# Attention and two perceptrons on one core: sums moved between the V products, q and k in one transfer, weights loaded earlier

## The chip, the cores and the metric

The kernel runs on one core of a Trainium2 chip. The metric is device time in microseconds (us) from launch to end. Most of the text speaks of the engines by their short names: PE multiplies matrices, ACT applies functions, DVE and POOL work element by element, SP only issues transfers.

## The reference

Multi-head attention with capped scores, whose output goes through two bias-free perceptrons, all in float32:

```python
batch, n_heads, seq, head_dim = (2, 12, 448, 64)
scores = scale * np.matmul(q, k.transpose(0, 1, 3, 2))
scores = cap * np.tanh(scores / cap)
attn = np.exp(scores - max)            # over the last axis
attn = attn / (np.sum(attn, axis=-1, keepdims=True) + 1e-09)
x = np.matmul(attn, v)                 # heads side by side: (896, 768)
h = x @ w_in;  g = relu(h) ** 2;       x = g @ w_out      # 768 -> 2048 -> 768
h = x @ w2_in; g = h * sigmoid(1.702 * h); out = g @ w2_out
```

The cap bounds the scores, so the kernel takes no maximum.

## The kernel before

**Attention, two heads at a time.** The 24 heads make 12 pairs. A pair's q and k stand transposed with one head on partitions 0 to 63 and the other on 64 to 127. For each pair the kernel makes the scores in three chunks of 128 keys (`scores`) and one of 64 (the first half of `tails`), takes tanh of each chunk (`tanh`, ACT) and one exponential over all of them (`exps`, ACT). The probabilities are multiplied with V chunk by chunk (`weigh`, three chunks c = 0, 1, 2, into the one bank `pv`; the second half of `tails` adds the 64 keys). The row sums come from POOL, which adds the chunks element by element (`add`, four instructions a pair), and from PE, which multiplies the result with a matrix of ones (`sum_up`, into the one bank `sm`). Pair 0 has no `add`: PE sums its chunks directly (`sum_all`). DVE then takes the reciprocal (`invert`, L415), multiplies (`normalise`, L419; it reads `pv`, and the next pair's `weigh` waits for that since there is one such bank) and cuts the result in a high and a low part (`split`, L90 and L93).

**Weights.** Each perceptron product is made of three passes over high and low parts of both factors (`mm3`, L102 to L104). The weights come in 64 blocks of 768 KB (`w.load`), and DVE and ACT turn each into a high and a low part: `magnitude`, `clamp`, `shift`, `low_word` (L151), `sign` (L158), then `high_part` and `low_part` (L90 and L93 on `wa`). The first two blocks are treated wholly inside attention, by `merge` and `parts` on DVE; the third is begun near its end. `w.sign` issues the load of a later block, since it frees the raw buffer.

**The order.** Each engine runs its instructions in the order in which they are written. In attention that order is a list of steps `at(t, fn, ...)`, sorted by the number t; t only sorts, it is no time that the chip keeps. A pair's steps lie PAIR = 6.7 apart. Transfers are issued by SP in the order of the code, but for a few by ACT at the start; a transfer whose buffer is still in use holds up those behind it on SP.

**Start.** ACT loads its function table at its first tanh (L434, on the tile `idle`); WARM matmuls on `idle` follow on PE; then pair 0's k and q arrive, one by SP and one by ACT, behind the tiny transfer of `cap`, from which DVE makes the scale `icap` that the first tanh reads.

**After attention.** `unit_a` for the first 448 rows and two blocks of w_in is run ahead inside attention (`ahead`), between the last pairs' products. Then PE works through 2304 matmuls of the perceptrons with few gaps.

Of the kernel before, what the change touches and what calls it, by code (L numbers as in the profile page):

```python
# [8 lines left out]
F32 = mybir.dt.float32  # L9
# [4 lines left out]
AF = mybir.ActivationFunctionType  # L14
# [5 lines left out]
P = 128  # L20
B, H, S, D = 2, 12, 448, 64
# [18 lines left out]


AHEAD = 2
WARM = 5

PAIR = 6.7


@with_exitstack
def attn_moe_moe(ctx, tc, qT, kT, v, cap, w1i, w1o, w2i, w2o, out):
    nc = tc.nc  # L50
    cp = ctx.enter_context(tc.tile_pool(name="cp", bufs=1))
    xp = ctx.enter_context(tc.tile_pool(name="xp", bufs=1))
# [12 lines left out]
    def sum_bank():  # L65
        return ps.tile([P, 512], F32, tag="sm", name="sm")
# [12 lines left out]
    def bank():  # L79
        return next(ring[0])  # L80
# [3 lines left out]
    def rnd(eng, out_, in_):  # L84
        if eng is nc.scalar:
            nc.scalar.activation(out_, in_, AF.Copy)  # L86
        elif eng is nc.gpsimd:
            nc.gpsimd.tensor_scalar(out_, in_, 1.0, 1.0, op0=ALU.mult, op1=ALU.mult)
        else:
            nc.vector.tensor_copy(out_, in_)  # L90
# [4 lines left out]
    def hi_lo(pool, tag):  # L95
        return (
            pool.tile([P, S], F32R, tag=f"{tag}_h", name=f"{tag}_h"),
            pool.tile([P, S], F32R, tag=f"{tag}_l", name=f"{tag}_l"),
        )
# [214 lines left out]
    def bounded_attention(w, cap_sb, actx):  # L314
        ap_ = actx.enter_context(tc.tile_pool(name="ap", bufs=2))
# [4 lines left out]
        idle = ap_.tile([P, 512], BF16, name="idle", bufs=1)  # L320
        otail = ap_.tile([P, P], F32, name="otail", bufs=1)
        kq, vv, raw, probs, total, sums, pvs, inverse = {}, {}, {}, {}, {}, {}, {}, {}
        halves = (slice(0, D), slice(D, P))
        rows = halves[::-1]

        def load_kq(i):
            b, n = divmod(i, H // 2)
            k = ap_.tile([P, S], F32, tag="k", name="k")
            q = ap_.tile([P, S], F32, tag="q", name="q")
            nc.sync.dma_start(k, kT[b, n])  # L330
            (nc.scalar if i == 0 else nc.sync).dma_start(q, qT[b, n])
            kq[i] = k, q

        def load_v(i):
            b, n = divmod(i, H // 2)
# [85 lines left out]
        def split(i):  # L421
# [3 lines left out]
            rest(nc.vector, ll, u, hh)  # L425
            x[i // 6, i % 6] = hh, ll

        nc.scalar.dma_start(cap_sb, bass.AP(tensor=cap.tensor, offset=cap.offset, ap=[[0, P], [1, 1]]))
        nc.vector.memset(idle, 0.0)
        nc.gpsimd.memset(ones, 1.0 + 1e-9)  # L430
        nc.gpsimd.memset(otail, 0.0)
        for h, r in zip(halves, rows):
            nc.gpsimd.memset(otail[r, h], 1.0 + 1e-9)
        nc.scalar.activation(idle[:, 0:1], idle[:, 1:2], AF.Tanh)  # L434
        warm = sum_bank()
        for _ in range(WARM):
            nc.tensor.matmul(warm, idle[:, :P], idle, start=True, stop=True)
        load_kq(0)
        nc.vector.tensor_scalar(bcap, cap_sb, -CAP_BOUND, CAP_BOUND, op0=ALU.max, op1=ALU.min)
        nc.vector.reciprocal(icap, bcap)  # L440
        nc.vector.tensor_scalar(icap, icap, 1.0 / 8.0, None, op0=ALU.mult)
        load_kq(1)
        w.load()
        load_v(0)

# [2 lines left out]
        def at(t, fn, *args):  # L448
            steps.append((t, fn, *args))

        n = NPR
        for i in range(n):
            t = PAIR * i
            if i > 1:
                at(t - 2 * PAIR + 2.5, load_kq, i)
            if i:
                at(t - 2 * PAIR + 10.3 if i > 2 else 2.6 + 0.2 * i, load_v, i)
            for c, d in enumerate((-5.1, -4.4, -3.7)):
                at(t + d, scores, i, c)
            for c, d in enumerate((-3.5, -3.4, -3.3, 1.0)):  # L460
                at(t + d, tanh, i, c)
            at(t + 3.1, exps, i)
            if i == 0:
                at(t + 6.6, sum_all, i, (0, 1))
                at(t + 8.2, sum_all, i, (2, 3))
            else:
                at(t + 6.6, add, i)
                at(t + {n - 2: 12.3, n - 1: 12.3}.get(i, 13.3), sum_up, i)
            for c, d in enumerate((12.2, 12.4, 12.5) if i == n - 1 else (11.05, 11.8, 12.5)):
                at(t + d, weigh, i, c)  # L470
            at(t + 14.0 if i else 10.4, invert, i)
            at(t + 17.2, normalise, i)
            at(t + 17.9, split, i)
        for i in range(-2, n):
            at(PAIR * i + 14.15 if i > -2 else -3.6, tails, i + 2 if i + 2 < n else None, i if i >= 0 else None)

        at(2.55, w.load)
        def merge(eng):
            w.magnitude(eng)
            w.clamp()  # L480
            w.shift()
            w.low_word()
            w.sign()
# [10 lines left out]
        at(4.0, merge, nc.vector)  # L494
        at(4.1, parts, nc.vector)
        at(9.7, merge, nc.vector)
        at(11.8, parts, nc.vector)
        end = PAIR * (n - 1)
        at(end + 13.0, begin)
        at(end + 13.0, w.low_word)  # L500
        at(end + 18.85, w.sign)
        at(end + 18.9, w.high_part, nc.scalar)
        at(end + 19.05, w.low_part)
# [19 lines left out]
    def general_attention(cap_sb, actx):  # L523
        ap_ = actx.enter_context(tc.tile_pool(name="gap", bufs=2))
        ident = ap_.tile([P, P], F32, name="ident", bufs=1)
        make_identity(nc, ident)
        mag = ap_.tile([P, 1], F32, name="mag", bufs=1)
        icap = ap_.tile([P, 1], F32, name="gicap", bufs=1)
        nc.vector.tensor_scalar(mag.bitcast(U32), cap_sb.bitcast(U32), 0x7FFFFFFF, None, op0=ALU.bitwise_and)
        nc.vector.reciprocal(icap, mag)  # L530
        nc.vector.tensor_scalar(icap, icap, 1.0 / 8.0, None, op0=ALU.mult)
        chunks = [(kc, slice(kc * P, min(S, (kc + 1) * P))) for kc in range(KC + 1)]
        for i in range(NPR):
            b, n = divmod(i, H // 2)
            kq = []
            for nm, src in (("k", kT), ("q", qT)):
                r = ap_.tile([D, 2, S], F32, tag=f"g{nm}", name=f"g{nm}")
                nc.sync.dma_start(r, src[b, n].rearrange("(e d) s -> d e s", e=2))
                kq.append(r)
            k, q = kq  # L540
            vm = ap_.tile([P, 2 * KC, D], F32, tag="gv", name="gv")
            nc.sync.dma_start(vm, v[b, n, :, :2 * KC])
            vl = ap_.tile([TL, 2, D], F32, tag="gvt", name="gvt")
            for e in range(2):
                nc.sync.dma_start(vl[:, e], v[b, n, D * (1 - e):D * (2 - e), 2 * KC])
            u = ap_.tile([P, S], F32, tag="gu", name="gu")
            for e in range(2):
                pT = ap_.tile([P, KC + 1, S], F32, tag="pT", name="pT")
                for qc in range(NC):
                    j = slice(qc * CP, (qc + 1) * CP)  # L550
                    sc = bank()
                    nc.tensor.matmul(sc[:CP, :S], q[:, 1 - e, j], k[:, 1 - e, :], start=True, stop=True)
                    t = ap_.tile([CP, S], F32, tag="gt", name="gt")
                    nc.scalar.activation(t, sc[:CP, :S], AF.Tanh, scale=icap[:CP])
                    m = ap_.tile([CP, 1], F32, tag="gm", name="gm")
                    nc.vector.tensor_reduce(m, t, axis=AX.X, op=ALU.max)
                    nc.vector.tensor_tensor(m, m, mag[:CP], op=ALU.mult)
                    nc.vector.tensor_scalar(t, t, mag[:CP], None, op0=ALU.mult)
                    nc.vector.tensor_scalar(t, t, m, None, op0=ALU.subtract)
                    nc.scalar.activation(t, t, AF.Exp)  # L560
                    s = ap_.tile([CP, 1], F32, tag="gs", name="gs")
                    nc.vector.tensor_reduce(s, t, axis=AX.X, op=ALU.add)
                    nc.vector.tensor_scalar(s, s, 1e-9, None, op0=ALU.add)
                    nc.vector.reciprocal(s, s)
                    nc.vector.tensor_scalar(t, t, s, None, op0=ALU.mult)
                    tp = bank()
                    for kc, jj in chunks:
                        nc.tensor.transpose(tp[:jj.stop - jj.start, kc * CP:(kc + 1) * CP], t[:, jj], ident[:CP, :CP])
                    nc.vector.tensor_copy(pT[:, 0:KC, j], tp[:, :KC * CP].rearrange("p (k q) -> p k q", k=KC))
                    nc.vector.tensor_copy(pT[:TL, KC, j], tp[:TL, KC * CP:S])  # L570
                pv = bank()
                for kc in range(KC):
                    nc.tensor.matmul(pv[:D, :S], vm[:, 2 * kc + e, :], pT[:, kc, :], start=kc == 0, stop=False)
                nc.tensor.matmul(pv[:D, :S], vl[:, e, :], pT[:TL, KC, :], start=False, stop=True)
                nc.scalar.activation(u[D * e:D * e + D, :], pv[:D, :S], AF.Copy)
            hh, ll = hi_lo(xp, f"x{b}_{n}")
            rnd(nc.gpsimd, hh, u)
            rest(nc.gpsimd, ll, u, hh)
            x[b, n] = hh, ll

    cap_sb = cp.tile([P, 1], F32, name="cap_sb")
    w = Weights()
# [8 lines left out]
    with tc.If(mag > CAP_BOUND_BITS):  # L591
        ring[0] = all_banks()
        w = Weights()
# [65 lines left out]
```

## Time and profile before

| | us |
|---|---|
| median of 3 runs | 575.86 |
| lowest and highest of them | 575.0 and 579.22 |
| the profiled execution's own time | 580.23 |
| its span, first to last instruction | 578.4 |
| mean granted PE clock | 0.992 of full |
| busy: PE, DVE, ACT, POOL | 557.5, 386.1, 258.8, 73.5 |

The busy shares are means over stages with different limits: POOL works in attention alone, and PE's busy time counts each matmul until its modelled end. The profiled execution is one run, and it is longer than all three of the timed ones. On PE a float32 matmul is recorded as two passes, so six instructions of the order stand as x12 in the profile.

### The profile page before, as it was taken

The page shows a single profiled execution, that of the slowest core. Times are in us where ns is not written, and L with a number is a line of the kernel's source. Part 1 is how long each engine was busy: PE and PEld are TensorE (multiplying, and loading weights), DVE is VectorE, ACT ScalarE, POOL GpSimd, SP SyncE. Part 2 cuts the span into 40 slices and gives each one's busy share as a digit, 9 for nine tenths or more (in the row PEclk, how much of TensorE's full clock was granted, in tenths as well). Part 3 has the DMA queues.
Part 4 walks back from the last instruction along what each step waited for, and adds up shares of the span by engine and source line. Part 5 has one row for each costly group of instructions (what it writes and reads, how often), then busy time and mean ns, then how long its engine had stood idle before and what let it go on. Part 6 is the DMA issues. An engine that isn't in the chain of part 4 may idle for free.

```text
span 578.4 us, 6902 instructions
## 1 busy us (share of the span) xinstructions
PE 557.5 (96%) x2753; PEld 463.6 (80%) x2753; DVE 386.1 (67%) x523; ACT 258.8 (45%) x333; POOL 73.5 (13%) x52
## 2 busy tenths in 40 slices
PE   6869999999999999999999999999999999999995
PEld 2323334689999999999999999999999999999995
DVE  4666666879988888653775367878888875366401
ACT  4948887055555554321332155555555522222101
POOL 0459999300000000000000000000000000000000
PEclk9979999999999999999999999999999999999999
DMA  5623330034433333431253123232323154154002
GB/s 169 233 86 96 95 97 17 1 110 124 150 109 110 109 110 109 164 110 54 94 179 110 54 98 120 97 123 91 128 83 136 54 172 148 63 199 150 22 0 101
DMA packets 16313, 61.87 MB, mean 107 GB/s; under 512 B 1936, under 2 KB 8080, under 8 KB 16272
## 3 DMA queue, kind: packets, MB, share of 16 engines
q1 hardware_dynamic: 15984, 61.12, 32.0%
q8 instruction: 23, 0.38, 0.3%
q10 hardware_dynamic: 288, 0.23, 0.1%
q14 instruction: 18, 0.15, 0.1%
HBM read 58.59 MB, written 2.75 MB: 106 GB/s over the span
## 4 chain that ended last, share of the span: by engine, by line
PE 86%; DVE 10%; DMA 2%; ACT 1%; issue 1%; SPq 0%; ACTq 0%; DVEq 0%
PE bb L102 19%; PE bb L104 19%; PE bb L103 19%; DVE r L415 5%; PE pv L379 5%; PE pv L103 3%; PE sm L104 3%; PE sm L102 3%; PE pv L104 3%; PE sm L103 3%; PE pv L102 3%; PE sm L396 2%; DMA wraw<-w1i 1%; DVE sm L419 1%; DVE wl L93 1%; DMA q<-qT 1%
## 5 line engine op out<-in xcount | busy, mean ns | idle before, releaser
L102 PE MATMUL bb<-x_l,wh 128*128 128x448 f32 x288 | 105.5, 366 | 0.0
L103 PE MATMUL bb<-x_h,wl 128*128 128x448 f32 x288 | 105.3, 366 | 0.0
L104 PE MATMUL bb<-x_h,wh 128*128 128x448 f32 x288 | 105.2, 365 | 0.0
L104 PE MATMUL bb<-g_h,wh 128*128 128x448 f32 x288 | 105.2, 365 | 0.0
L102 PE MATMUL bb<-g_l,wh 128*128 128x448 f32 x288 | 105.2, 365 | 0.0
L103 PE MATMUL bb<-g_h,wl 128*128 128x448 f32 x288 | 105.2, 365 | 0.0
L86 ACT ACTIVATE wh<-wa 128x768 fp32r<-128x768 f32 x62 | 52.4, 846 | 100.0 <-PE bb L104 45.2
L93 DVE TENSOR_TENSOR wl<-wa,wh 128x768 fp32r<-128x768 f32 x64 | 63.8, 997 | 46.2 <-ACT wh L86 46.1
L132 ACT ACTIVATE wa<-wraw 128x768 f32<-128x768 f32 x62 | 56.6, 913 | 70.2 <-DVE wl L93 16.9
L158 DVE SCALAR_TENSOR_TENSOR wa<-wraw,wa 128x768 uint32<-128x768 uint32 x64 | 62.8, 981 | 1.0
L151 DVE SCALAR_TENSOR_TENSOR wa<-wraw,wa 128x768 uint32<-128x768 uint32 x64 | 60.9, 952 | 0.1
L102 PEld LDWEIGHTS bb<-x_l,wh 128*128 128x128 f32 x288 | 54.1, 188 | 6.4 <-issue 1.4
L103 PEld LDWEIGHTS bb<-x_h,wl 128*128 128x128 f32 x288 | 54.1, 188 | 4.7 <-DVE wl L93 0.4
L104 PEld LDWEIGHTS bb<-x_h,wh 128*128 128x128 f32 x288 | 54.1, 188 | 4.3
L104 PEld LDWEIGHTS bb<-g_h,wh 128*128 128x128 f32 x288 | 54.1, 188 | 4.3
L103 PEld LDWEIGHTS bb<-g_h,wl 128*128 128x128 f32 x288 | 54.1, 188 | 4.3
L102 PEld LDWEIGHTS bb<-g_l,wh 128*128 128x128 f32 x288 | 54.1, 188 | 4.2
L86 ACT ACTIVATE g_h<-gt 128x448 fp32r<-128x448 f32 x64 | 37.0, 578 | 45.5 <-DVE gt L199 44.4
L199 DVE TENSOR_TENSOR gt<-bb,gt 128x448 f32<-128x448 f32 x48 | 29.8, 621 | 36.5 <-ACT gt L195 23.0
L415 DVE RECIPROCAL r<-sm 128x448 f32<-128x448 f32 x12 | 35.5, 2956 | 22.6 <-PE sm L396 22.5
L140 DVE TENSOR_SCALAR wa<-wa 128x768 f32<-128x768 f32 x64 | 35.5, 555 | 12.4 <-ACT wa L132 12.2
L93 DVE TENSOR_TENSOR g_l<-gt,g_h 128x448 fp32r<-128x448 f32 x64 | 39.7, 620 | 4.2 <-ACT g_h L86 3.9
(84 smaller groups left out, 734.0 us busy)
## 6 DMA issues: line engine op xcount, KB each, us to landing
wraw<-w1i SPq DMA_DIRECT2D x16, 768.0 KB, 4.3
wraw<-w1o SPq DMA_DIRECT2D x16, 768.0 KB, 4.3
wraw<-w2i SPq DMA_DIRECT2D x16, 768.0 KB, 4.2
wraw<-w2o SPq DMA_DIRECT2D x16, 768.0 KB, 4.2
k<-kT SPq DMA_DIRECT2D x12, 224.0 KB, 2.6
v<-v SPq DMA_DIRECT2D x12, 224.0 KB, 3.6
outT<-o SPq DMA_DIRECT2D x12, 224.0 KB, 3.1
q<-qT SPq DMA_DIRECT2D x11, 224.0 KB, 2.7
```

What stands on the lines that cost most here:

```text
L86: nc.scalar.activation(out_, in_, AF.Copy)
L93: eng.tensor_tensor(out_, in_, hi, op=ALU.subtract)
L102: nc.tensor.matmul(ps, wh, xl, start=first, stop=False)
L103: nc.tensor.matmul(ps, wl, xh, start=False, stop=False)
L104: nc.tensor.matmul(ps, wh, xh, start=False, stop=last)
L132: nc.scalar.activation(a.bitcast(F32), raw[:, :, 1].bitcast(F32), AF.Abs)
L140: nc.vector.tensor_scalar(af, af, LOW, HIGH, op0=ALU.max, op1=ALU.min)
L151: nc.vector.scalar_tensor_tensor(a, raw[:, :, 0], 29, a, op0=ALU.logical_shift_right, op1=ALU.bitwise_or)
L158: nc.vector.scalar_tensor_tensor(a, raw[:, :, 1], 0xC0000000, a, op0=ALU.bitwise_and, op1=ALU.bitwise_or)
L199: nc.vector.tensor_tensor(gt, ps, gt, op=ALU.mult)
L379: nc.tensor.matmul(pvs[i][h, :S], vv[i][:, 2 * c + e, :], t[:, 2 * c + e, :], start=c == 0, stop=False)
L415: nc.vector.reciprocal(r, sums[i][:, :S])
```

## The change

The edits are these.

- **q and k in one array.** The host stacks q and k, so that a pair's q and k come in one transfer of 448 KB instead of two of 224 KB. Pair 0's comes in two halves by partitions, one by SP and one by ACT, and is now issued ahead of `cap`.
- **Table load and warm-up.** The first tanh, which loads the table, now writes one column of pair 1's q and k buffer, so pair 1's transfer waits for it, and the warm-up matmuls wait only for the memset of `idle`. There are seven of them instead of five.
- **Weights earlier.** The second block of weights is loaded at the start, right behind the first, and its `parts` stand at 9.75 instead of 11.8, before the first `invert`.
- **Sums between the chunks.** `sum_up` stands at 12.3 for every pair but the last, between `weigh` of c = 1 and c = 2, instead of at 13.3 behind all three (pair 10 had 12.3 already); for the last pair at 12.0, ahead of all three.
- **Last low word.** `low_word` of the third block moves behind the last pair's `split`.

```diff
-WARM = 5
+WARM = 7
...
         def load_kq(i):
-            k = ap_.tile([P, S], F32, tag="k", name="k")
-            q = ap_.tile([P, S], F32, tag="q", name="q")
-            nc.sync.dma_start(k, kT[b, n])
-            (nc.scalar if i == 0 else nc.sync).dma_start(q, qT[b, n])
-            kq[i] = k, q
+            t = ap_.tile([P, 2, S], F32, tag="qk", name="qk")
+            if i == 0:
+                for eng, h in zip((nc.sync, nc.scalar), halves):
+                    eng.dma_start(t[h], qk[b, n, h])
+            else:
+                if i == 1:
+                    nc.scalar.activation(t[:, 0, 0:1], idle[:, 1:2], AF.Tanh)
+                nc.sync.dma_start(t, qk[b, n])
+            kq[i] = t[:, 1], t[:, 0]
...
+        nc.vector.memset(idle, 0.0)
+        load_kq(0)
         nc.scalar.dma_start(cap_sb, bass.AP(tensor=cap.tensor, offset=cap.offset, ap=[[0, P], [1, 1]]))
-        nc.vector.memset(idle, 0.0)
...
-        nc.scalar.activation(idle[:, 0:1], idle[:, 1:2], AF.Tanh)
         warm = sum_bank()
         for _ in range(WARM):
             nc.tensor.matmul(warm, idle[:, :P], idle, start=True, stop=True)
-        load_kq(0)
+        load_kq(1)
...
-        load_kq(1)
+        w.load()
         w.load()
         load_v(0)
...
-                at(t + {n - 2: 12.3, n - 1: 12.3}.get(i, 13.3), sum_up, i)
+                at(t + (12.0 if i == n - 1 else 12.3), sum_up, i)
...
-        at(2.55, w.load)
...
-        at(11.8, parts, nc.vector)
+        at(9.75, parts, nc.vector)
...
-        at(end + 13.0, w.low_word)
+        at(end + 18.8, w.low_word)
```

On DVE, from the end of the second block's `merge` to pair 0's `normalise`, before (`wa`, `wh`, `wl` are a weight block and its parts, `r` the reciprocal):

```order
L158 SCALAR_TENSOR_TENSOR wa<-wraw,wa 128x768
L415 RECIPROCAL r<-sm 128x448
L90 CAST wh<-wa 128x768
L93 TENSOR_TENSOR wl<-wa,wh 128x768
L419 TENSOR_TENSOR sm<-pv,r 128x448
```

The same place with the change:

```order
L158 SCALAR_TENSOR_TENSOR wa<-wraw,wa 128x768
L90 CAST wh<-wa 128x768
L93 TENSOR_TENSOR wl<-wa,wh 128x768
L420 RECIPROCAL r<-sm 128x448
L424 TENSOR_TENSOR sm<-pv,r 128x448
```

The two instructions of `parts` have passed the reciprocal; both still stand ahead of `normalise`.

On PE, one middle pair from its product with V to the scores of a later pair, before (`s` is POOL's sum):

```order
L379 MATMUL pv<-t,v 64x448 x6
L396 MATMUL sm<-s,ones 64x448 x2
L355 MATMUL bb<-q,k 64x448 x2
L358 MATMUL pv<-t,v 64x448 x2
L348 MATMUL bb<-q,k 128x448 x6
```

The same pair with the change:

```order
L384 MATMUL pv<-t,v 64x448 x4
L401 MATMUL sm<-s,ones 64x448 x2
L384 MATMUL pv<-t,v 64x448 x2
L360 MATMUL bb<-qk 64x448 x2
L363 MATMUL pv<-t,v 64x448 x2
L353 MATMUL bb<-qk 128x448 x6
```

The two sums have passed the last chunk's two products; what follows keeps its place.

On SP, from the start to the third pair's q and k (the fourth in the change), before:

```order
L330 DMA k<-kT 128x448 x2
L331 DMA q<-qT 128x448
L123 DMA wraw<-w1i 128x1536
L337 DMA v<-v 128x448
L589 TENSOR_LOAD bits
L589 ISA x2
L330 DMA k<-kT 128x448
L331 DMA q<-qT 128x448
L123 DMA wraw<-w1i 128x1536
```

The same stretch with the change:

```order
L331 DMA qk<-qk 64x896
L336 DMA qk<-qk 128x896
L123 DMA wraw<-w1i 128x1536 x2
L342 DMA v<-v 128x448
L336 DMA qk<-qk 128x896
L342 DMA v<-v 128x448 x2
L123 DMA wraw<-w1i 128x1536
```

The second weight block no longer stands behind pair 2's q and k, whose buffer PE must first free.

## Rows read from the trace of the kernel before

**Rows 1.** Waits of PE, whole run: engine, line, releaser: us in total, times, longest

```profile
PE pv L379 <- DVE sm L419: 8.8, 9, 5.1
...
PE pv L103 <- DVE wl L93: 0.3, 1, 0.3
```

**Rows 2.** Windows, busy time of the engines in two stretches, then granted clock

```profile
32.90:42.00 9.10, 8.61 (x38) 2.97 (x40) 4.92 (x5) 2.92 (x2) 3.63 (x3) 0.78 0.21 60
...
105.00:112.00 7.00, 7.00 (x36) 3.71 (x35) 6.71 (x7) 0.00 (x0) 0.89 (x1) 1.00 0.00 0
```

**Rows 3.** Timeline of the start: start, length, engine, instruction, idle time before it

```profile
0.75 0.40 ACTq L428 DMA_DIRECT2D cap_sb<-cap  x1
...
0.88 0.27 DVE L429 MEMSET idle<- 128x256 uint32 x1 [0.88 <-PEq L647]
...
2.74 2.31 PE L437 MATMUL sm<-idle 128*128 128x512 bf16 x5 [2.74 <-ACT idle L434]
...
5.01 0.15 DVE L439 TENSOR_SCALAR bcap<-cap_sb 128x1 f32<-128x1 f32 x1 [3.86 <-DMA cap_sb<-cap]
...
6.37 4.10 PE L348 MATMUL bb<-q,k 64*128 64x448 f32 x12 [1.31 <-DMA q<-qT]
...
8.27 1.01 ACT L367 ACTIVATE t<-bb,icap 128x896 f32<-128x896 f32 x1 [5.59 <-PE bb L348]
8.65 0.56 DVE L134 TENSOR_SCALAR wa<-wraw 128x768 uint32<-128x768 uint32 x1 [3.11 <-DMA wraw<-w1i]
...
13.02 0.96 DVE L93 TENSOR_TENSOR wl<-wa,wh 128x768 fp32r<-128x768 f32 x1
```

**Rows 4.** DMA issues: KB each, median us from issue to landing

```profile
k<-kT SPq DMA_DIRECT2D x12, 224.0 KB, 2.6
...
q<-qT ACTq DMA_DIRECT2D x1, 224.0 KB, 5.0
```

**Rows 5.** Chain that ended last, 12 to 37 us: start, length, what

```profile
12.27 7.11 DMA wraw<-w1i
...
22.18 2.74 DVE wa L158
24.92 2.87 DVE r L415
...
28.53 3.81 DVE wl L93
...
32.93 4.42 PE pv L379 x12
```

**Rows 6.** Timeline of POOL, first instruction of the first and the second add

```profile
21.68 2.42 POOL L386 TENSOR_TENSOR s<-t 128x896 f32<-128x896 f32 x1 [20.24 <-ACT t L372]
...
29.44 2.07 POOL L386 TENSOR_TENSOR s<-t 128x896 f32<-128x896 f32 x1
```

**Rows 7.** Chain that ended last, one period of the middle pairs

```profile
41.94 2.48 PE pv L379 x12
44.41 0.80 PE sm L396 x4
45.24 2.97 DVE r L415
48.30 0.64 DVE sm L419
```

**Rows 8.** Timeline, an exponential and the POOL add that reads it

```profile
46.78 2.91 ACT L372 ACTIVATE t<-t,bcap 128x3136 f32<-128x3136 f32 x1
...
49.82 2.09 POOL L386 TENSOR_TENSOR s<-t 128x896 f32<-128x896 f32 x1 [0.37 <-POOL s L389]
```

**Rows 9.** POOL's groups from 49.5 to 99.1 us, seven adds: busy, mean ns, idle before

```profile
L389 POOL TENSOR_TENSOR s<-s,t 64x448 f32<-64x448 f32 x14 | 16.0, 1140 | 1.1
L386 POOL TENSOR_TENSOR s<-t 128x896 f32<-128x896 f32 x7 | 14.7, 2098 | 2.6 <-POOL s L389 2.6
L387 POOL TENSOR_TENSOR s<-s,t 128x896 f32<-128x896 f32 x7 | 14.6, 2081 | 0.6
```

More of the change, by code (lines that the diff above doesn't have):

```diff
@@ L42, with attn_moe_moe @@
 AHEAD = 2
-WARM = 5
+WARM = 7
 PAIR = 6.7
 @with_exitstack
-def attn_moe_moe(ctx, tc, qT, kT, v, cap, w1i, w1o, w2i, w2o, out):
+def attn_moe_moe(ctx, tc, qk, v, cap, w1i, w1o, w2i, w2o, out):
     nc = tc.nc
@@ L535, in general_attention @@
             kq = []
-            for nm, src in (("k", kT), ("q", qT)):
+            for nm, m in (("k", 1), ("q", 0)):
                 r = ap_.tile([D, 2, S], F32, tag=f"g{nm}", name=f"g{nm}")
-                nc.sync.dma_start(r, src[b, n].rearrange("(e d) s -> d e s", e=2))
+                nc.sync.dma_start(r, qk[b, n, :, m].rearrange("(e d) s -> d e s", e=2))
                 kq.append(r)
@@ L637 @@
     arrays = {
-        "qT": pairs(inputs["q"]),
-        "kT": pairs(inputs["k"]),
+        "qk": c(np.stack([pairs(inputs["q"]), pairs(inputs["k"])], axis=3)),
         "v": chunks(inputs["v"]),
```

## The prediction

> **What bounds the kernel now.** I read PE's waits first, since PE is busy for 96% of the span and what remains is to be had where it stands still. One line holds nearly all of it: the product with V waits nine times for DVE's `normalise` (L419), 8.8 us in total, 5.1 of them once [rows 1]. Next come the windows, for what a long wait does to PE. In the stretch behind the 5.1 the granted clock is 0.78, where it is 1.00 at the end of attention [rows 2]: part of that stretch ran at 1.2 instead of 2.4 GHz after PE had stood still. The last window also shows PE busy in 7.00 of 7.00 us, so near the end of attention nothing but PE's own work is left. The chain of waits then says what lies behind the two kinds of wait.
>
> The long one [rows 5]: the second weight block is issued at 12.27 and takes 7.11 to land, so DVE gets to its `merge` at 19.4, and then two of its weight instructions are stretched, L158 to 2.74 and L93 to 3.81. Undisturbed, that L93 takes 0.96 [rows 3], and L158 works on a block of the same size. Both stretches lie beside POOL's adds, which run from 21.68 on [rows 6]. Pair 0's reciprocal lies between them, its `normalise` behind both, and PE resumes at 32.93. There pair 1's product takes 4.42, against 2.48 later [rows 5, 7], which is the low clock.
>
> The short ones, eight of together 3.7, so 0.46 each, are one closed loop: product 2.48, sum 0.80, reciprocal 2.97, `normalise` 0.64, which with the gaps between is 7.05 a pair [rows 7]. PE's own work in it is 7.05 - 0.46 = 6.6. POOL is close behind: seven adds take 16.0 + 14.7 + 14.6 busy and 1.1 + 0.6 between their instructions, so 45.3 + 1.7 = 47.0, or 6.71 each; the other 2.6, or 0.37 an add, is idle time ahead of L386 [rows 9]. The row names POOL's own add as releaser, but the exponential ends at 46.78 + 2.91 = 49.69 and L386 starts at 49.82 [rows 8], so POOL waits for ACT there and has that much to spare.
>
> **Part by part.** *Start.* Now the first scores start at 6.37, behind q, which came 5.0 after its issue on the same queue behind `cap`, and the first tanh at 8.27 [rows 3, 4]. With the change both halves of q and k are issued first, at about 0.75, when `cap` goes out now [rows 3]. They land 2.6 (a k or q in mid-run) to 5.0 (q now) later [rows 4], at 3.4 to 5.8; I take 4.4, since half of what was moved ahead of q is gone. Seven warm-up matmuls take 7 x 0.43 (five run in 2.31, the last one's end included [rows 3]) = 3 us and start once `idle` is set, at 0.88 + 0.27 = 1.15 [rows 3], so they end at 4.2 and cost nothing; if the data came at 3.4 they would cost 0.8. Scores to tanh is 8.27 - 6.37 = 1.9, which gives 6.3. But the first tanh needs `cap` too, which comes at 5.01 now and stands behind a half of q and k with the change. Issued 0.5 later and as long in flight, with 4 x 0.15 for the four tiny DVE instructions behind it [rows 3], it gives 6.1; if it lands 1.4 behind that half, as q landed behind it (5.01 to 6.37), 6.4 to 7.8. I take the tanh at 6.9: **-1.4**, with bounds of 0 and -2.2. Whether the clock rises earlier is open and inside these bounds. All of attention hangs on that tanh, so the gain is carried on.
>
> The Trainium skill, in SBUF — State Buffer, section "Can I just issue two DMAs to hit both halves?", speaks against this edit: two transfers at once, on partitions from 0 and from 64, measured only 6% above a single one, and 64 partitions get 196 GB/s where 128 get 328. Estimated from that page, two halves of 224 KB would take 2.3 us one behind the other against 1.4 for the whole, so the data, and `cap` behind them, would come 0.9 later and the time be 565.7 instead of 564.8. No row here shows a transfer over half of the partitions.
>
> *Second block and `parts`.* The table load now stands behind two transfers on ACT, about 0.4 later, so the tanh that it serves ends near 3.1 instead of 2.7 [rows 3]; SP then issues pair 1's q and k, block one at 3.6 and block two at 4.0. Block one arrives at 8.65 now [rows 3]; at worst it takes 7.11 as block two does [rows 5], so 10.7; I take 9.2. A block takes from 8.65 to 13.02 + 0.96, so 5.33, on DVE [rows 3]. Both are done at 9.2 + 10.7 = 19.9, and L93, the last of them, starts 0.96 before that. POOL's first add starts at 21.68 - 1.4 = 20.3. So the weight work is over before POOL begins, and the two stretches, some 1.8 and 2.85, go. The reciprocal of pair 0 then ends at about 23 and `normalise` follows at about 24; PE reaches pair 1's product at 32.93 - 5.1 - 1.4 = 26.4. If block one came at 10.7, L93 would start at 20.4 and might be held for the 2.42 of POOL's instruction; the reciprocal would end at 26.8, which costs 1 us. So the wait goes, **-5.1**, and with it the low clock, 4.42 - 2.48, **-1.9**. What is late next there is PE itself.
>
> *Sums between the chunks.* No instruction is added. The sum starts 0.83 earlier (a third of 2.48), so the loop is 7.05 - 0.83 = 6.22, below PE's 6.6, and the eight waits go: -3.7. The new wait is PE's for POOL's add, with the last chunk, the tails, the next scores and so ACT queued behind it. POOL needs 6.71 a pair, 0.11 above PE; over the seven middle pairs that is 0.8, less what slack it starts with. Behind these, the first unit that is run ahead lets POOL catch up. I take 0.7 back: **-3.0**, with bounds of -3.7 and 0. A transfer of 448 KB instead of 2 x 224 KB has a whole pair of time to land; cost 0, and the issues that it saves are SP's, which no engine waits for here.
>
> *End.* The last sum comes ahead of the product, but PE goes through it without a gap [rows 2], so nothing is gained there. `low_word` moves from a wait of DVE to behind the split: 0.96 more (as L93 on a block) ahead of the third block's parts, of which the earlier reciprocal gives back about 0.65. PE waits 0.3 already for the fourth block's low part [rows 1], so what is late adds to it: **+0.3**, bounds 0 and 0.96.
>
> The sum is -1.4 - 5.1 - 1.9 - 3.0 + 0.3 = -11.1. Against the profiled execution's own time that is 580.23 - 11.1 = 569.1. That execution is 4.37 above the median and above all three timed runs, so one of its terms, the low clock perhaps, need not be whole in the others; I keep the sum for the median: **575.86 - 11.1 = 564.8**.
>
> **Rivals.** *The start gains nothing.* `cap`, or the later half, comes no sooner than q does now. For it: `cap`, of a few bytes, took from 0.75 to 5.01 [rows 3], and with the change it queues behind 224 KB. Against it: q stood behind it and still was there by 6.37. 564.8 + 1.4 = 566.2.
>
> *The pace stays at 7.05.* POOL or ACT takes the place of the loop. For it: POOL has only 0.37 of slack [rows 9]. Against it: that 0.37 is a wait for ACT, whose exponential hangs on PE, which comes earlier. 564.8 + 3.0 = 567.8.
>
> *The long wait stays.* DVE's weight work falls beside POOL again. This takes a second block that lands after 20.3 - 5.3 = 15.0, so 11 us in flight, where the row has 7.11 [rows 5]. Left are -1.4 - 3.0 + 0.3 = -4.1: 571.8.
>
> *POOL sets a slower pace.* PE now stands at each sum until POOL is done, with all else of the pair behind it. The first add took 29.44 - 21.68 = 7.76 [rows 6], beside DVE's weight work. Were all adds like it, ten pairs would lose 0.71 each, 7.1, against 1.4 + 7.0 - 0.3 = 8.1 won before: 574.9, no change. From 7.86 an add on the kernel is slower than before; if the shorter pair doubled the stretch of 1.05, to 8.8, it would lose 17.5 and come to 585.3. Against it: seven adds in a row beside DVE's reciprocals and splits took 6.71 [rows 9], and no weight work is left beside them until the end.
>
> **How the numbers follow.** Chances: the forecast 0.66, no gain at the start 0.14, pace of 7.05 0.08, long wait stays 0.07, POOL at 7.76 0.03, POOL beyond 7.86 0.02. About 1%, 5.8 us, is what a measurement of this kernel tells from no change. The first three are faster by more than that, but for a small tail; the long wait at 571.8 and POOL at 7.76 are within it. So faster 0.86, same 0.12, slower 0.02. The range: all terms at their good ends give -2.2 - 7.0 - 3.7 = -12.9, so 563.0, and 1.5 lower for the spread of the runs, 561.5. Above it takes in both small rivals together, 564.8 + 1.4 + 3.0 = 569.2, and the low clock's part that a run may lack, to 570.5.
>
> **What would show it.** In the profile after: the first tanh near 6.9; L93 of the second block at about 1.0; no wait of PE for `normalise` above 0.1, and a granted clock of 1.00 from there on; recurring sums near 6.7 apart, with small waits of PE for POOL in their place; the perceptrons starting about 11 us earlier and running at the same pace. It would be wrong if POOL's adds grew, if a new idle stretch of PE brought the low clock back, or if the perceptrons' first blocks of weights came late and gave the gain back there.

## The result and the profile after

| | us |
|---|---|
| before, median of 4 | 575.56 (575.0 to 579.22) |
| the change, median of 4 | 569.07 (567.71 to 577.35) |
| ratio | 0.987, 95% interval 0.9822 to 0.9919 |
| ratio when timed again beside 23 runs of before | 0.9845, 0.9786 to 0.9905 |
| profiled execution: own time, span, granted clock | 568.3, 566.5, 0.997 |

The forecast was 564.8 in a range of 561.5 to 570.5: the time lies inside it, 4.3 above the point. The two profiled executions differ by 580.23 - 568.3 = 11.9, near the sum of 11.1; the medians differ by 6.5. In some executions of most kernels here PE takes 2% longer over each matmul at a granted clock of 1.00 (244 instead of 249 in 50 us, in the second look at the change), some 9 us in all; these are left out below, and a median is one of the others.

All waits of PE in the changed kernel, to be held against [rows 1] (in total, times, longest):

```profile
PE sm L410 <- ACT t L377: 1.4, 1, 1.4
PE sm L442 <- DVE idle L433: 1.2, 1, 1.2
PE bb L103 <- DVE wl L93: 0.3, 1, 0.3
PE pv L103 <- DVE wl L93: 0.3, 1, 0.3
```

The nine waits for `normalise` are gone, the long one and the short ones; L103's 0.3 is there twice instead of once. The timeline of the start and of pair 0's end, as [rows 3] and, for L93 and the product, [rows 5]:

```profile
1.20 3.17 PE L442 MATMUL sm<-idle 128*128 128x512 bf16 x7 [1.20 <-DVE idle L433]
...
4.30 4.31 PE L353 MATMUL bb<-qk 64*128 64x448 f32 x12
...
5.21 0.15 DVE L444 TENSOR_SCALAR bcap<-cap_sb 128x1 f32<-128x1 f32 x1 [4.07 <-DMA cap_sb<-cap]
...
6.95 2.85 ACT L372 ACTIVATE t<-bb,icap 128x896 f32<-128x896 f32 x3 [3.47 <-PE bb L353]
...
10.35 2.91 ACT L377 ACTIVATE t<-t,bcap 128x3136 f32<-128x3136 f32 x1
...
18.64 0.96 DVE L93 TENSOR_TENSOR wl<-wa,wh 128x768 fp32r<-128x768 f32 x1
19.51 2.95 DVE L420 RECIPROCAL r<-sm 128x448 f32<-128x448 f32 x1
...
19.81 2.09 POOL L391 TENSOR_TENSOR s<-t 128x896 f32<-128x896 f32 x1 [18.37 <-ACT t L377]
...
23.55 0.63 DVE L424 TENSOR_TENSOR sm<-pv,r 128x448 f32<-128x448 f32 x1 [1.09 <-PE pv L363]
...
25.84 1.72 PE L384 MATMUL pv<-t,v 128*64 128x448 f32 x8
```

The first tanh comes at 6.95, L93 of the second block takes 0.96 and is over when POOL begins at 19.81, and pair 1's product starts at 25.84 instead of 32.93, with nothing in front of it. The chain of waits, one period as in [rows 7], and the window that answers to [rows 2]:

```profile
39.04 1.65 PE pv L384 x8
40.69 0.86 PE sm L401 x4
41.55 0.75 PE pv L384 x4
43.22 2.46 PE bb L353 x12
45.67 1.65 PE pv L384 x8
```

```profile
32.90:42.00 9.10, 9.10 (x52) 3.63 (x48) 5.76 (x6) 8.74 (x9) 8.87 (x6) 1.00 0.27 88
```

A period is 45.67 - 39.04 = 6.63, DVE has left the chain, and the granted clock is 1.00 where it was 0.78. At the end of attention the timeline shows the last sum ahead of the last product, and the start of the perceptrons (L102):

```profile
94.79 0.97 PE L401 MATMUL sm<-s,ones 128*64 128x448 f32 x4
...
98.84 0.47 PE L102 MATMUL bb<-x_l,wh 128*128 128x448 f32 x1
```

Before, the perceptrons start 12.4 later:

```profile
111.23 0.47 PE L102 MATMUL bb<-x_l,wh 128*128 128x448 f32 x1
```

From there to the last instruction the trace takes 566.5 - 98.84 = 467.7, and before 578.4 - 111.23 = 467.2. So all that is won is won ahead of the perceptrons, and 0.5 is given back in them.

### The profile page after: what moved, and what is told of

Same layout as the page of the kernel before. It is cut to its first block, busy times and chain, and to the rows that moved or that the text cites. A ratio compares the mean times of both kernels' runs of the same rounds, so it can differ in the third digit from the quotient of the medians.

```text
span 566.5 us, 6891 instructions
## 1 busy us (share of the span) xinstructions
PE 556.7 (98%) x2755; PEld 465.5 (82%) x2755; DVE 381.1 (67%) x523; ACT 259.1 (46%) x333; POOL 71.4 (13%) x52
## 4 chain that ended last, share of the span: by engine, by line
PE 95%; DVE 2%; ACT 2%; issue 0%; DVEq 0%
PE bb L102 20%; PE bb L103 20%; PE bb L104 20%; PE pv L384 5%; PE bb L353 5%; PE pv L103 3%; PE sm L103 3%; PE sm L104 3%; PE pv L104 3%; PE sm L102 3%; PE pv L102 3%; PE bb L360 2%; PE sm L401 2%; PE sm L410 1%; PE sm L442 1%; ACT t L377 1%
## 5 line engine op out<-in xcount | busy, mean ns | idle before, releaser
L103 PE MATMUL bb<-x_h,wl 128*128 128x448 f32 x288 | 105.3, 366 | 0.3 <-DVE wl L93 0.3
L102 PE MATMUL bb<-x_l,wh 128*128 128x448 f32 x288 | 105.5, 366 | 0.0
L103 PE MATMUL bb<-g_h,wl 128*128 128x448 f32 x288 | 105.2, 365 | 0.0
L102 PE MATMUL bb<-g_l,wh 128*128 128x448 f32 x288 | 105.2, 365 | 0.0
L93 DVE TENSOR_TENSOR wl<-wa,wh 128x768 fp32r<-128x768 f32 x64 | 61.0, 953 | 48.3 <-ACT wh L86 48.2
L158 DVE SCALAR_TENSOR_TENSOR wa<-wraw,wa 128x768 uint32<-128x768 uint32 x64 | 61.1, 955 | 1.1
L151 DVE SCALAR_TENSOR_TENSOR wa<-wraw,wa 128x768 uint32<-128x768 uint32 x64 | 61.0, 953 | 0.1
L102 PEld LDWEIGHTS bb<-x_l,wh 128*128 128x128 f32 x288 | 54.1, 188 | 6.4 <-issue 1.4
L103 PEld LDWEIGHTS bb<-x_h,wl 128*128 128x128 f32 x288 | 54.1, 188 | 5.0 <-DVE wl L93 0.7
L103 PEld LDWEIGHTS bb<-g_h,wl 128*128 128x128 f32 x288 | 54.1, 188 | 4.3
L102 PEld LDWEIGHTS bb<-g_l,wh 128*128 128x128 f32 x288 | 54.1, 188 | 4.3
L93 DVE TENSOR_TENSOR g_l<-gt,g_h 128x448 fp32r<-128x448 f32 x64 | 39.8, 621 | 3.9 <-ACT g_h L86 3.7
```

The costliest lines, as they stand in the source:

```text
L93: eng.tensor_tensor(out_, in_, hi, op=ALU.subtract)
L102: nc.tensor.matmul(ps, wh, xl, start=first, stop=False)
L103: nc.tensor.matmul(ps, wl, xh, start=False, stop=False)
L151: nc.vector.scalar_tensor_tensor(a, raw[:, :, 0], 29, a, op0=ALU.logical_shift_right, op1=ALU.bitwise_or)
L158: nc.vector.scalar_tensor_tensor(a, raw[:, :, 1], 0xC0000000, a, op0=ALU.bitwise_and, op1=ALU.bitwise_or)
```

## The experiments

Theory A, formed on the result: the long wait at pair 1 (5.1, and 1.9 of low clock) is a matter of some executions, the profiled one of before among them, and the median holds little of it. Theory B: it is in all of them, and the change gives gain back elsewhere. The experiments also undo the change's parts one by one.

**The kernel before, again.** No edit.

> The kernel before, unchanged, to see how far its executions differ. Its first profiled execution took 580.23, its timed runs 575.0 to 579.22, and the change won 11.9 in the profiles but about 7 in the medians. Theory A (the long wait varies): in an ordinary execution the second weight block lands earlier against POOL's adds, so this profile has an own time near 575.5, and the longest wait of PE for normalise is 1 to 3 us instead of 5.1, perhaps with a granted clock of 1.00 behind it. Theory B (the gain is given back elsewhere): this profile shows the same wait of 5.1 again, and where its time is near 575.5 the perceptrons are shorter than in the first profile by 4 us.

Own time 579.0. The chain of waits:

```profile
13.29 6.52 DMA wraw<-w1i
...
22.62 2.85 DVE wa L158
...
29.09 1.78 DVE wl L93
...
31.46 4.17 PE pv L379 x12
```

The wait is 2.8 this time, the low clock is there. Its length hangs on one step: L93 takes 1.78 here and 3.81 in [rows 5]. What POOL did beside it, in the timeline:

```profile
27.50 2.55 POOL L389 TENSOR_TENSOR s<-s,t 64x448 f32<-64x448 f32 x2
30.01 2.80 POOL L386 TENSOR_TENSOR s<-t 128x896 f32<-128x896 f32 x1
```

Here L93 got through between two POOL instructions, and the POOL instruction behind it became long, 2.80 against 2.09. The profile fits neither theory as it was put: the wait is shorter than 5.1, and the time is not near 575.5. The step that tells the theories apart is in the times. Every run comes with its mean granted clock, and before's runs over all jobs fall into two lots: 27 at a clock of 0.997 or 0.998, which took 574.3 to 576.4 (median 575.2), and 28 at 0.992 to 0.996, which took 577.2 to 582.6. The profiled executions of 580.23 and 579.0 belong to the second, and their traces tell how far one fell: 0.992 goes with the wait of 5.1, 0.995 with that of 2.8. Of the 28, 17 are at 0.992 or 0.993 (median 581.7) and 10 at 0.995 or 0.996 (median 578.7). The stretch at half clock at pair 1's wait (0.50 between 32 and 34 us in both traces) is what sets these traces apart from 0.998; so half of the executions do not seem to fall to the low clock there. That speaks for theory A.

**The change, again.** No edit.

> The changed kernel, unchanged, for a closer ratio. Theory A: 567.5 to 569, ratio 0.986 to 0.989, and the same trace as the first time: no wait of PE for normalise above 0.1, perceptrons from 98.8 on. Theory B: the ratio is the same, but the profile shows perceptrons that differ by several us between the two looks.

Ratio 0.9845. Its executions, seven with the first three, have a median of 567.9 (567.55 to 569.83) and a clock of 0.996 to 0.999: one lot. The trace of its profiled one (577.79) has no wait for `normalise` either, the scores wait 1.0 for q and k, and the perceptrons start at 99.68. The ordinary executions of before are 575.2 - 567.9 = 7.3 longer, the others 9 to 15.

**Weights back.**

```diff
-        w.load()
         w.load()
         load_v(0)
...
+        at(2.55, w.load)
...
-        at(9.75, parts, nc.vector)
+        at(11.8, parts, nc.vector)
```

> The change with its weight edit undone: the second block is loaded behind pair 2's q and k again, and its parts stand behind pair 0's reciprocal. Theory A: the block lands near 17, its L158 and L93 run beside POOL's adds again and take up to 2.7 and 3.8, and PE waits 3 to 5 us for pair 0's normalise, with a lower clock behind it if the wait is long: 571.5 to 575. Rival (the wait belonged to the late start, not to the weights): with the earlier start and the earlier sums normalise is in time, and it is within 1 us of the change, 568 to 569.

Median 568.4 of five, ratio 0.985, within 0.5 of the change: so the rival was right. The timeline of DVE, and POOL's first add:

```profile
15.96 0.56 DVE L134 TENSOR_SCALAR wa<-wraw 128x768 uint32<-128x768 uint32 x1 [1.66 <-DMA wraw<-w1i]
...
18.77 1.00 DVE L158 SCALAR_TENSOR_TENSOR wa<-wraw,wa 128x768 uint32<-128x768 uint32 x1
...
23.33 2.72 DVE L93 TENSOR_TENSOR wl<-wa,wh 128x768 fp32r<-128x768 f32 x1
25.97 0.62 DVE L424 TENSOR_TENSOR sm<-pv,r 128x448 f32<-128x448 f32 x1
```

```profile
20.77 2.11 POOL L391 TENSOR_TENSOR s<-t 128x896 f32<-128x896 f32 x1 [19.33 <-ACT t L377]
```

With the earlier start the block lands at 15.96 even in its old place, 3.4 earlier than in [rows 5]: it is issued at 11.01 instead of 12.27, and it is in flight for 5.0 instead of 7.1. L158 is through a microsecond before POOL begins, L93 alone is stretched, and `normalise` starts at 25.97, in time for PE.

**Sums back.**

```diff
-                at(t + (12.0 if i == n - 1 else 12.3), sum_up, i)
+                at(t + {n - 2: 12.3, n - 1: 12.3}.get(i, 13.3), sum_up, i)
...
-        at(end + 18.8, w.low_word)
+        at(end + 13.0, w.low_word)
```

> The change with the sums put back behind the last chunk, and the last low word back ahead of the last reciprocal. Theory A: the closed loop of 7.05 a pair is back, PE waits 0.45 for normalise in each of eight or nine pairs, and it is 2.5 to 4 us slower than the change: 571 to 572.5. Rival (POOL or ACT sets the pace anyway): the pace stays near 6.65 and the time within 1 us of the change.

Median 572.3 of eleven, ratio 0.9921: 4.4 slower than the change. PE's line of waits for `normalise` is back without its long member:

```profile
PE pv L384 <- DVE sm L424: 4.1, 8, 0.9
```

**Start back.** As in the kernel before, `cap` goes first, the table load is on `idle` with five warm-up matmuls behind it, pair 0's k and q come apart, and pair 1's transfer does not wait.

```diff
+                nc.sync.dma_start(t[:, 1], qk[b, n, :, 1])
+                nc.scalar.dma_start(t[:, 0], qk[b, n, :, 0])
...
+        nc.scalar.activation(idle[:, 0:1], idle[:, 1:2], AF.Tanh)
         warm = sum_bank()
```

> The change with its start undone: the scale's transfer first, the table load on the idle tile, five warm-up matmuls behind it, then pair 0's k by SP and q by ACT; pair 1's q and k do not wait for the table. Weights and sums stay as in the change. Theory A: the first tanh comes near 8.3 instead of 6.95, exp of pair 0 at 12.2 instead of 10.35, and all behind it 1.4 to 1.9 later: 569.5 to 570.5. Rival (the start is covered by something later): within 0.5 us of the change.

Median 571.1 of eight, 3.2 slower than the change, more than theory A allowed. The timeline:

```profile
6.84 4.75 PE L350 MATMUL bb<-qk 64*128 64x448 f32 x12 [1.78 <-DMA qk<-qk]
...
13.21 2.91 ACT L374 ACTIVATE t<-t,bcap 128x3136 f32<-128x3136 f32 x1
```

The exponential comes at 13.21, in the change at 10.35. The scores start 2.5 later and take 4.75 instead of 4.31, where the twelve of a later pair take 2.53. One matmul of these first scores takes up to 1.11 us against 0.54 later, though the granted clock is recorded as 1.00 in both stretches.

**Parts back, load early.** Only `at(9.75, parts, ...)` becomes `at(11.8, parts, ...)`.

> The change with only the place of the second block's parts put back, behind pair 0's reciprocal; the block is still loaded at the start. Theory A says that the load is what counts: DVE gets through merge by 18, the reciprocal ends near 21, L93 is stretched beside POOL to at most 3.8 and normalise starts by 25.5, just when PE is ready: 0 to 1 us slower than the change, 568 to 569.5. Rival (the place counts): L93 is held so long that PE waits 2 us or more for normalise: 570 to 573.

Median 567.2 of four, 0.7 below the change, and no wait for `normalise`: the place of `parts` is worth nothing here.

**Pair 0 whole.** One transfer of 448 KB by SP.

```diff
-            if i == 0:
-                for eng, h in zip((nc.sync, nc.scalar), halves):
-                    eng.dma_start(t[h], qk[b, n, h])
-            else:
-
-                if i == 1:
...
-                nc.sync.dma_start(t, qk[b, n])
+            nc.sync.dma_start(t, qk[b, n])
```

> The change with pair 0's q and k in one transfer of 448 KB by SP over all partitions instead of two halves by SP and ACT; the scale's transfer is then alone on ACT's queue. If two halves of the partitions are slow, as the Trainium skill's SBUF page has it, the scores start earlier than 4.3 by some tenths, limited by the warm-up that ends at 4.3: 0 to 0.5 us faster than the change. If they are not, q and k land together later, as a 448 KB transfer does in mid-run (3.3 us), near 4.5 to 5: 0.2 to 0.8 us slower.

Only one of its executions can be compared, 568.28, so its time decides nothing. Its timeline does more for the start:

```profile
6.20 2.80 ACT L367 ACTIVATE t<-bb,icap 128x896 f32<-128x896 f32 x3 [3.52 <-PE bb L348]
...
19.02 2.09 POOL L386 TENSOR_TENSOR s<-t 128x896 f32<-128x896 f32 x1 [17.58 <-ACT t L372]
19.16 2.77 DVE L93 TENSOR_TENSOR wl<-wa,wh 128x768 fp32r<-128x768 f32 x1
```

The first tanh comes at 6.20 instead of 6.95. But the start of the change has other executions too: 7.34 in its second look, 7.16 and 7.11 with the weights or the sums back, and 6.30 with the parts back, so 0.75 is not a price of the halves. And with POOL starting at 19.02, L93 falls beside it and is stretched, so that PE waits 0.5 for `normalise`.

**No wait for the table.** The first tanh writes a tile of its own instead of pair 1's buffer.

```diff
-                if i == 1:
-                    nc.scalar.activation(t[:, 0, 0:1], idle[:, 1:2], AF.Tanh)
...
+        nc.scalar.activation(tiny, idle[:, 1:2], AF.Tanh)
         warm = sum_bank()
```

> The change without the wait of pair 1's q and k for the table load: the first tanh writes a tile of its own. Pair 1's q and k and the weights go out some 1.5 us earlier and share the DMA engines with pair 0's. If that wait is worth something, pair 0's data come later than 4.3 and the first tanh later than 6.95, up to 1.5 us slower than the change. If not, DVE's weight work starts up to 1 us earlier, which nobody waits for: the same time.

Median 568.1 of four, as the change. The scale comes at 6.49 instead of 5.21, and the tanh, now behind it, at 7.12, within the 6.30 to 7.34 of the executions that have the wait; pair 0's scores start at 4.30, as in the change. So the wait shields `cap`, and nothing of that shows in the time.

**One more look at before.** No edit.

> One more look at the kernel before. Its timed runs gather near 575 and, less often, near 579, its two profiles so far are of the second kind (580.23 with a wait of 5.1, 579.0 with 2.8, the product behind them at a low clock in both). Theory A (the wait is in some executions only): if the own time is near 575, no wait for normalise is above 1 us and the product of pair 1 takes 2.5 instead of over 4; if it is 578 to 580, a wait of 2.5 to 5 stands there. Theory B (the wait is in all): a wait of 3 to 5 also in an execution near 575.

The time, 588.49, is not compared; this look tells of the wait alone: 5.0, at a clock of 0.991. All three profiles of before show a long wait, and none of an execution near 575 was taken, so what theory A says of these rests on their times and clocks.

**Before, with the weights alone.** The weight edit of the change and nothing else.

> The kernel before with the weight edit alone: the second block is loaded at the start and its parts stand ahead of pair 0's reciprocal. Theory A: this removes only the executions near 579; the ordinary ones stay where they are, 574.5 to 575.5, ratio 0.993 to 1.00 depending on how many runs of before have the wait. Theory B: the wait of 3 to 5 goes from all executions, 569 to 571.5.

Median 574.6 of twelve, all between 573.4 and 575.2 with clocks of 0.996 to 0.999. PE's waits:

```profile
PE pv L379 <- DVE sm L419: 4.0, 8, 0.9
```

The long wait is gone and the slower lot with it: none of twelve, where it was half. The ordinary executions gain 0.6. As theory A has it.

**Before, with the sums alone.** The line of `sum_up` and that of `low_word` of the change.

> The kernel before with the sums between the chunks alone (and the last low word behind the split). If the three edits add up without overlap, the sums alone win what putting them back cost, 4: 570.5 to 571.5 in the ordinary executions, pace 6.6 to 6.7 a pair. If a long wait at pair 1 stays and covers part of it: 572 to 575.

Seven executions at a clock of 0.997 or 0.998 took 571.1 to 573.2, median 572.4; four at 0.992 to 0.995 took 575.3 to 578.6; the twelfth, at 0.990, took 581.1. The profile, 578.14, is of the second lot:

```profile
PE pv L379 <- DVE sm L419: 5.0, 1, 5.0
```

The eight short waits are gone, the long one stands alone: the two kinds have separate causes.

**Whole pair 0, parts behind the split.** The edit of the whole pair, and `at(18.0, parts, nc.vector)`.

> A version that may beat both: the change with pair 0's q and k in one transfer, which brought the first tanh to 6.2 instead of 6.95, and with the second block's parts behind pair 0's split, since beside POOL's first add, which then starts at 19.0, L93 was stretched to 2.8 ahead of the reciprocal. Expected: no wait of PE for normalise, 0.5 to 1 us faster than the change, 566.8 to 567.5. If the parts now hold up pair 1's reciprocal, a wait of PE of 0.5 or more stands one pair later and it is no faster than the change.

Median 568.0 of six (567.7 to 568.2), ratio 0.9849: not faster than the change, though its trace has no wait for `normalise` either. No version beat the change clearly.

## Why the prediction was right, and what was mis-sized

**The long wait, -5.1 and -1.9.** The mechanism was right: the late block, the two stretched instructions, the fall of the clock. In the change, L93 of the second block ends at 18.64 + 0.96 = 19.60, 0.2 ahead of POOL's first add; forecast were 19.9 and 20.3. Its share of the median was wrong, and this is the term that was mis-sized most. The prediction said that "one of its terms, the low clock perhaps, need not be whole in the others" and then kept the sum for the median. It is nearly the whole -7.0 that half of the executions do not have: removing this wait alone gains 0.6 in the ordinary ones, and 3 to 8 in the others. The warning stood in the first table: the profiled execution was 4.37 above the median and above all timed ones.

That the time lies in the range is in part luck. With 0.6 for this term the forecast would have been 564.8 + 6.4 = 571.2, above the range; the start and the sums were worth more than forecast, and that brought the time back into it.

**Why the wait comes and goes** is shown in part. POOL and DVE hold each other up: L93 took 0.96 ahead of POOL, and 1.78, 2.72, 2.77 and 3.81 beside it, and POOL's L386 took 2.42 and 2.80 instead of 2.09. The Trainium skill, SBUF — State Buffer, section "Who interferes with whom", says the same: a DVE instruction with two SBUF inputs and a POOL instruction that reads SBUF take a shared port in turn, each for its whole length, and whichever starts first goes first. The traces agree on the turns, but not on who is next: L93, held from 28.53 on [rows 5], let POOL's L386 of 29.44 [rows 6] go ahead at its full pace of 2.07; in the second look, held from 29.09 on, it went ahead of the one of 30.01. That is most of the step from a wait of 5.1 to one of 2.8. The second block had landed 2.3 to 2.4 before POOL's first add in the three executions with a wait of 5.0 or 5.1, and 2.7 before it in the one with 2.8. That a still longer lead spares the ordinary executions fits this, but was not seen in a profile; that they are spared is inferred from the clocks and from the weight edit's alone.

**The weights.** The edit to which the prediction gave the -7.0 is not needed for it beside the others: with the start moved, the old place of the block does about as well (568.4). The prediction let each part act alone and did not ask whether the earlier start frees pair 2's buffer earlier and so brings the block forward by itself. It does: with the weights back, pair 2's transfer goes out at 10.64 instead of 11.41 and the block behind it at 11.01 instead of 12.27. Why the block is then 2.1 shorter in flight is open. In the kernel before, the weight edit alone removes the wait.

**The start, -1.4.** Mis-sized: undoing it costs 3.2. The tanh came at 6.95, as forecast (6.9), which is in part luck, since other executions of this start have it at 6.30 to 7.34. What the prediction did not see is that the step from the first tanh to the exponential is no constant. Pair 0's scores took 3.47 to 4.85 in five profiled executions with the new start and 3.90 to 4.75 in six with the old one, and the exponential came at 9.66 to 11.72 and at 12.05 to 13.21. The profile of before, with 4.10 and 12.22, was one of its quicker ones, so the usual start is slower than the one that was read. These exponentials are 1.8 apart in the mean and the medians of the times 3.2; between the two the size stays open, and so does what sets the pace of the first scores.

**The sums, -3.0.** Undoing them costs 4.4 in the medians, above the bound of 3.7, and alone in the kernel before they gain 575.2 - 572.4 = 2.8. The traces lie between: from pair 1's product to the perceptrons it takes 98.84 - 25.84 = 73.0 in the change and 76.7 with the sums back as well as in the kernel before with the weights alone, so 3.7. The price of POOL was right, 0.1 a pair. Early in the change, POOL not yet in the way, a period of PE is 32.44 - 25.91 = 6.53, where the prediction took 6.6:

```profile
25.91 1.65 PE pv L384 x8
27.57 0.75 PE sm L401 x4
28.32 0.75 PE pv L384 x4
29.98 2.46 PE bb L353 x12
32.44 1.65 PE pv L384 x8
```

Later it is 6.63, with 0.86 for the sum instead of 0.75. POOL's adds follow each other at 6.63 there with no idle time ahead of L391, and an add ends (47.16) where the sum behind it starts (47.16): POOL now sets the pace. The list of waits does not show it.

**The end, +0.3.** One more wait of 0.3 for a block's low part, as said; the perceptrons as a whole take 0.5 longer in the trace.

Put together for ordinary executions: 3.2 for the start and 4.4 for the sums, where the whole is 7.3. The medians come from lots that spread over 1.4 to 3.1 us, so the 0.3 between tells nothing, and the weights lie in it. Of the rivals, the start that gains nothing, the pace of 7.05 and the long wait that stays are ruled out by the trace, and no POOL add in the middle grew.

**The page on halves.** With one transfer over all partitions the scores could start at 4.48 and 4.51 in two executions; of the two halves the later one landed at 4.95 to 5.36 in six. The estimate that the prediction worked out from the Trainium skill, SBUF — State Buffer, section "Can I just issue two DMAs to hit both halves?", and from the rates in its section "Door 1: The DMA port swizzle (why `[64,N]` ≈ `[32,N]`)", was 0.9. The traces agree that the whole is earlier, by 0.4 to 0.9. At the first tanh the two overlap, 6.20 and 6.42 against 6.30 to 7.34, and in the median it did not show: the whole-pair version with late parts takes 568.0 against 567.9.

## What to carry to other kernels

Before a profile's wait is priced into a median, set the profiled execution's time beside the timed ones: a profile that is slower than all of them may show a stall that only some have, and the granted clock of each run tells which. Price edits to one stage together, since an earlier start can bring the next transfer forward and take over another edit's gain. In a closed loop between two engines, it pays to move the work that the other engine waits for ahead of work that nobody waits for: two instructions in another place took 3.7 us out of attention here.

## What was not expected

A POOL and a DVE instruction that meet cost one of them up to the rest of one instruction of the other and the whole of the next, and which one loses changes from run to run: in the second look at before, DVE's L93 lost only 0.8 and POOL's next instruction 0.7; in the first, L93 lost 2.85, more than a POOL instruction of 2.09. Behind a stand of 2.8 us as behind one of 5.1 PE fell to half clock (0.50 granted): the product behind it took 4.17 and 4.42 instead of 2.48.
